# Fused causal attention and gated projection: shared output blocks, two V tiles, and new engine orders

## The chip, the cores and the metric

The kernel runs on one core of a Trainium2 chip. Its time is the device time of one execution in microseconds (us), given as the median of several runs. The engines are named as in the profile: PE does the matmuls (PEld is its weight load), DVE, ACT and POOL are the vector, scalar and GpSimd engines, and SP issues the DMAs.

## What is computed

There are 8 batches of 8 heads, 576 positions and 64 elements per head, all in float32. Attention is causal with a decay along the positions, and its result x (576 x 512 per batch) goes through a gate: a causal convolution of 5 taps per channel, a sigmoid, a product with x @ w_val, and a last projection with w_out.

```python
cum = np.cumsum(np.maximum(s, 0.0), axis=-1)
scores = q @ k.T / 8 + np.minimum(-(cum[:, None] - cum[None, :]), 0.0)   # causal
attn = exp(scores) / sum(exp(scores));  x = attn @ v                      # heads side by side
gate = sigmoid(sum(conv_w[k] * xp[k:k + S] for k in range(5)))
out = (gate * (x @ w_val)) @ w_out
```

## The kernel before

The work goes by batch b and, in a batch, by pair p of heads; n = 4b + p counts the 32 pairs. Since the decay is a difference of two terms, the part of the key is taken into V: Vp = V * w with w = exp(cum - half the total), and the part of the query falls out in the division by the sum, which is one more column of Vp.

For each batch q and k are loaded (L515; positions 512 to 575 separately as "tail", L523), cast to bf16 (L518), transposed on PE (L557, tail L546) and evacuated into QKT (L561, L549). For each pair come three score steps (L566), each with an exponential of 128x1024 on ACT (L592), and for the last 64 queries one small step per batch (exp4, L578); POOL masks the diagonal (L598, L603). Attention times Vp is L613; DVE takes the reciprocal of the sums (L618) and scales to xn (L623); PE transposes (L631) and DVE or ACT copies to xT (L635). The four older taps of the convolution, divided by the weight of the newest (the "ratios", L496 to L507), are added one by one into gp, on DVE (L647, L649) or on POOL (L644, L645). ACT takes the tanh (L653). PE does x @ w_val by halves of 288 positions and chunks of 128 channels (L660), DVE multiplies with the gate into glu (L666), PE does the last projection by blocks of positions (L672, function outp), ACT or DVE copies the block to ot (L677), and SP stores it (L680).

576 positions are four and a half blocks of 128. The kernel computes five blocks of 128 per batch, the last two overlapping (WIN, L221), and stores only the upper 64 rows of one of them: 40 blocks in all, each of four matmuls over the chunks.

V is loaded into one float32 tile, vst, in a frame whose 65th columns are 1 (L420 to L422): batch 0 by pairs of heads (L532), the others by five position blocks (L538). A load for batch b waits until the four Vp products of batch b - 1 have read the tile (L716, L717).

The order on every engine is written by a planner in the program (class Plan, L256). Each task is added with an engine, a cost in us, a key, the tasks that it needs, and the buffers that it takes and gives back. The planner runs these through a list schedule and emits the instructions in that order, so each engine's queue is fixed before the launch. Keys come from a table of offsets (DUE, L226), and for tasks that two engines can do a string of digits picks one (CHOICE, L246):

```python
t = T["xe", n] = add(("DVE", "ACT"), (0.37, 0.65), n + due("xe"), lambda e, n=n: x_evac(e, n), [t],
                     pick=("xe", n))
```

Score tasks have PE mode "R" (64 rows of the array), all others "N"; STAY (L244) is a key penalty for leaving a mode. For SP the planner lets an issue take 0.06 us and counts the transfers one after another (L352 to L355). Buffers in turn: P 3, gp 2, th 6, ot 3, qkf 3 (L389), and 8 PSUM banks.

At the end of the program a small count decides whether a general path (not taken for these inputs) is run.

Of the kernel before, what the change touches and what calls it, by code (L numbers as in the profile page):

```python
# [205 lines left out]
def pcol(kb, qb):  # L206
    if kb == qb:
        return kb * 128
    if qb == 4:
# [16 lines left out]
DUE = dict(w=-69.33, lwv=-4.26, lwo=-2.61, cwv=56.85, cwo=86.75, av=-11.07, norm=-74.98, xt=-16.64,  # L226
           xe=-86.49, tap=14.23, dtap=-1.47, tanh=-72.16, val=7.76, dval=0.88, out=11.28, dout=0.61,
           oute=87.55, qt=-4.79, qe=133.25, tt=-0.4, te=-149.08, s4=-20.03, vp=-7.1, cast=76.15, lqk=-1.56,
           mask=-123.76, lv=-49.38, av_e=7.71, av_l=6.68, cast_e=-31.51, cast_l=0.54, dout_e=-1.01,
           dout_l=-28.82, dtap_e=-7.57, dtap_l=16.17, dval_e=0.26, dval_l=0.84, lqk_e=-7.13, lqk_l=48.32,  # L230
           lv_e=98.37, lv_l=-92.01, mask_e=11.67, mask_l=11.41, norm_e=50.24, norm_l=38.99, out_e=0.39,
           out_l=42.92, oute_e=70.67, oute_l=-23.24, qe_e=-66.52, qe_l=-3.56, qt_e=4.39, qt_l=0.95,
           s4_e=8.96, s4_l=-14.16, tanh_e=58.9, tanh_l=56.45, tap_e=3.56, tap_l=-27.97, te_e=47.36,
           te_l=62.72, tt_e=19.75, tt_l=0.79, val_e=-3.44, val_l=-1.96, vp_e=-68.8, vp_l=29.32, xe_e=13.94,
           xe_l=0.22, xt_e=-5.82, xt_l=-13.61)


def due_of(b, name):
# [5 lines left out]
STAY = (0.1, 54.75)  # L244

CHOICE = dict(vp0="0100",  # L246
              cast="12200210",
              wts="00",
              te="10001100",
              qe="10100010000000001000100000100010",  # L250
              xe="00100010001000010000000000010010",
              tap="00000000100000000000001000000000000000010000100000000000000010000000000000001000001000001000100000000010000010010010001101110000",
              oute="1000001110101000010100010100011010000010")


class Plan:  # L256
# [22 lines left out]
    def run(self):  # L279
# [33 lines left out]
        while len(self.order) < len(self.tasks):  # L313
            started, later = False, []
            for e in engs:
# [36 lines left out]
                if e == "SP":  # L352
                    idle_at[e] = now + 0.06
                    dma_free = max(dma_free, now + 1.2) + us
                    t["done"] = dma_free + 0.8  # L355
                else:
                    idle_at[e] = t["done"] = now + us
# [21 lines left out]
def main_path(ctx, tc, q, k, v, s, moe_w_val, moe_conv_w, moe_w_out, out, okcnt):  # L379
# [9 lines left out]
    plan = Plan(dict(P=3, gp=2, th=6, ot=3, qkf=3))  # L389
# [30 lines left out]
    vst = one.tile([128, NKB, 8, 65], FP32, name="vst")  # L420
    nc.gpsimd.memset(vst[:, :, :, 64:65], 1.0)
    nc.gpsimd.memset(vst[0:64, 4, :, :], 0.0)  # L422
# [12 lines left out]
    glus = two("glu", [128, 4, S], BF16)  # L435
# [35 lines left out]
    t = add("DVE", 0.65, -8, relu, [t_s])  # L471
    t = add("DVE", 1.3, -8, total, [t])
    t = add("DVE", 0.75, -8, centre, [t])
# [20 lines left out]
    t = add("SP", 0.3, -8.95, lambda: nc.sync.dma_start(out=cw, in_=moe_conv_w))  # L494
    t = add("PE", 0.3, -6, conv_T, [t], take=[("bank", "cw")])
# [11 lines left out]
    t_cw = add("DVE", 1.2, -6, ratios, [t], give=[("bank", "cw")])  # L507
# [18 lines left out]
    def vprime(eng, b, p):  # L526
        h = slice(2 * p, 2 * p + 2)
        eng.tensor_tensor(Vps[b % 2][:, :, h], vst[:, :, h],  # L528
                          w[:, :, b * 8 + 2 * p:b * 8 + 2 * p + 2].unsqueeze(3).to_broadcast([128, NKB, 2, 65]),
                          ALU.mult)  # L530

    def load_v_pair(p):  # L532
        for h in (2 * p, 2 * p + 1):
            nc.sync.dma_start(out=vst[:, 0:4, h, 0:64], in_=v[0, h, 0:512, :].rearrange("(i p) d -> p i d", i=4))  # L534
        nc.sync.dma_start(out=vst[64:128, 4, HP[p], 0:64],
                          in_=v[0, HP[p], 512:576, :].rearrange("h s d -> s h d"))

    def load_v_block(b, i):  # L538
        n = kbs[i]
        nc.sync.dma_start(out=vst[128 - n:128, i, :, 0:64],  # L540
                          in_=v[b, :, kbo[i]:kbo[i] + n, :].rearrange("h s d -> s h d"))
# [127 lines left out]
    def outp(b, i):  # L669
        ps = slot["o", b, i] = bank(("o", b, i), 128, DM)  # L670
        for c in range(4):
            nc.tensor.matmul(ps, glus[b % 2][:, c, WIN[i]:WIN[i] + 128], wo[:, c, :], start=(c == 0), stop=(c == 3))  # L672

    def out_evac(e, b, i):
        r = slice(128 - kbs[i], 128)
        ot = slot["ot", b, i] = work("ot", (b, i), [128, DM], FP32)
        copy[e](ot[r, :], slot["o", b, i][r, :])  # L677

    def store(b, i):
        nc.sync.dma_start(out=out[b, kbo[i]:kbo[i] + kbs[i], :], in_=slot["ot", b, i][128 - kbs[i]:128, :])  # L680

    for b in range(B):
# [4 lines left out]
        if b == 0:  # L687
            t_tl = add("SP", 1.45, -8.4, lambda: load_tail(0))
            t_tail = T["tailc", 0] = add("DVE", 0.45, -6, lambda: nc.vector.tensor_copy(tailbs[0], tails[0]), [t_tl])
            for p in range(4):  # L690
                for wh in range(2):
                    def ld(p=p, wh=wh):
                        f = slot["f", 0, wh, p] = one.tile([128, 2, 256], FP32, name=f"first{p}{wh}")
                        dma_qk(0, wh, HP[p], f)
                    t = add("SP", 0.82, -8.5 + 0.5 * p + wh * 0.01, ld)
                    T["cast", 0, wh, p] = add(("DVE", "ACT", "POOL"), (0.32, 0.5, 0.8), p - 9, lambda e, p=p, wh=wh: cast_qk(
                        copy[e], 0, wh, HP[p], slot["f", 0, wh, p]), [t], pick=("cast", 2 * p + wh))
                t = add("SP", 1.45, -8.3 + 0.5 * p, lambda p=p: load_v_pair(p))
                T["vp", 0, p] = add(("DVE", "POOL"), (0.85, 1.25), p - 2, lambda e, p=p: vprime(
                    nc.vector if e == "DVE" else nc.gpsimd, 0, p), [t, t_w], pick=("vp0", p))  # L700
        else:
            fs = []
            for wh in range(2):
                def ld(b=b, wh=wh):
# [3 lines left out]
                c = add("POOL", 1.95, n0 + due("cast"), lambda b=b, wh=wh: cast_qk(  # L708
                    nc.gpsimd.tensor_copy, b, wh, slice(0, 8), slot["f", b, wh]),
                    [t] + [T.get(("qt", b - 2, p)) for p in range(4)], give=[("qkf", (b, wh))])  # L710
                for p in range(4):
                    T["cast", b, wh, p] = c
            t = add("SP", 1.45, n0 + due("lqk") + 0.5, lambda b=b: load_tail(b), [T.get(("tailc", b - 2))])
            t_tail = T["tailc", b] = add("POOL", 0.7, n0 + due("cast") + 0.3, lambda b=b: nc.gpsimd.tensor_copy(
                tailbs[b % 2], tails[b % 2]), [t, T.get(("tt", b - 2))])
            ts = [add("SP", 1.45, n0 + due("lv") + i * 0.01, lambda b=b, i=i: load_v_block(b, i),  # L716
                      [T["vp", b - 1, p] for p in range(4)]) for i in range(NKB)]  # L717
            for p in range(4):
                T["vp", b, p] = add("POOL", 1.25, n0 + p + due("vp"), lambda b=b, p=p: vprime(nc.gpsimd, b, p),
                                    ts + [t_w, T.get(("av", b - 2, p))])  # L720

        old_s = ([T.get(("s4", b - 2, 3))] + [T.get(("s", n0 - 8 + p, i)) for p in range(4) for i in range(3)])
        t = T["tt", b] = add("PE", 0.25, n0 + due("tt") if b else -6.5, lambda b=b: tail_T(b), [t_tail] + old_s,
                             take=[("bank", ("tt", b))])
        t_te = add(("ACT", "DVE"), (0.49, 0.6), n0 + due("te") if b else -6.3, lambda e, b=b: tail_evac(e, b), [t],
                   give=[("bank", ("tt", b))], pick=("te", b))
        for p in range(4):
            t = T["qt", b, p] = add("PE", 0.45, n0 + p + due("qt") if b else p - 6.9, lambda b=b, p=p: qk_T(b, p),
                                    [T["cast", b, 0, p], T["cast", b, 1, p]] + old_s, take=[("bank", ("qt", b, p))])
            T["qe", b, p] = add(("ACT", "DVE"), (0.9, 1.15), n0 + p + due("qe") if b else p - 6.8,  # L730
# [3 lines left out]
        for ps_ in ([[p] for p in range(4)] if b == 0 else [[0, 1, 2, 3]]):  # L734
# [7 lines left out]
            t = add("POOL", 0.15 + 0.11 * n, n0 + ps_[0] + due("mask"), lambda b=b, ps_=ps_: mask4(b, ps_), [t])  # L742
# [131 lines left out]
```

## Time and profile before

| | |
|---|---|
| median of 5 runs | 210.34 us (209.94 to 214.14) |
| the profiled execution | 209.82 us, its span 208.0 us |
| granted clock of PE, mean | 0.973 |
| PE busy | 174.1 us (84%) |
| DVE busy | 176.3 us (85%) |
| ACT busy | 163.3 us (78%) |
| POOL busy | 162.3 us (78%) |
| moved by DMA | 40.48 MB, 195 GB/s over the span |

The profile is of one execution. A row of a group gives a line of the kernel, the engine and operation, what it writes and reads with the shape of the tile, how many, and then busy us and mean ns of one. A wait is idle time of an engine ahead of an instruction, put down to what ended it. Some rows that are used later, of copies from PSUM and of the output matmuls:

| row | count | mean ns |
|---|---|---|
| L635 DVE, xT copy 128x576 | 26 | 449 |
| L635 ACT, the same | 6 | 661 |
| L561 DVE, QKT evacuation 128x1024 | 7 | 1217 |
| L561 ACT, the same | 25 | 1046 |
| L677 ACT, output copy 128x512 | 20 | 589 |
| L677 DVE, the same | 12 | 682 |
| L644 + L645 POOL, one tap | 18 | 1142 + about 1400 |
| L647 DVE, one tap | 85 | 803 |
| L672 PE, output matmul 128x512 | 141 recorded of 160 | 379 (four take 0.97 us back to back) |

### The profile page before, as it was taken

Reading aid. Unit: us, or ns where it says so; the run is one execution under the profiler, and the core shown is the slowest. Engines: PE = TensorE matmul, PEld = TensorE weight load, DVE = VectorE, ACT = ScalarE, POOL = GpSimd, SP = SyncE. Lnnn points to the kernel's source line nnn. Section 1 sums busy time; section 2 is a strip of 40 time slices with the busy share of each in tenths; the row PEclk is TensorE's granted clock in tenths of the full one; section 3 lists DMA queues with packets and bytes.
Section 4 is the critical chain, followed back from the end, with each engine's and each line's share of the span. In section 5 each row is a group of like instructions: output and inputs, shape, how many; then the busy total and the mean of one; then the engine's idle time right before and its main releaser. Section 6 shows DMA issues by size and latency. Waiting matters only on the chain.

```text
span 208.0 us, 6007 instructions
## 1 busy us (share of the span) xinstructions
PE 174.1 (84%) x2392; PEld 119.0 (57%) x2411; DVE 176.3 (85%) x311; ACT 163.3 (78%) x205; POOL 162.3 (78%) x179
## 2 busy tenths in 40 slices
PE   1598796799879997789899799989899999979950
PEld 0356584575637765467665657565576556745620
DVE  3728979999986998579999999999999998999810
ACT  2379779978997999987996997899987998553330
POOL 4276695899959987999499999958975899999300
PEclk9999969999978999999999999999999999999995
DMA  4999999999999999969997911941159120222551
GB/s 135 238 274 307 367 181 198 363 269 243 228 347 277 271 236 301 313 217 231 350 341 171 203 62 28 198 135 54 50 120 228 65 79 0 104 101 76 181 184 59
DMA packets 69230, 40.48 MB, mean 195 GB/s; under 512 B 47109, under 2 KB 63493, under 8 KB 69194
## 3 DMA queue, kind: packets, MB, share of 16 engines
q1 hardware_dynamic: 69194, 40.01, 73.0%
q8 instruction: 21, 0.34, 0.7%
q14 instruction: 15, 0.12, 0.2%
HBM read 30.57 MB, written 9.44 MB: 192 GB/s over the span
## 4 chain that ended last, share of the span: by engine, by line
DVE 29%; PE 26%; ACT 24%; issue 8%; SPq 5%; DMA 3%; POOL 2%; ACTq 0%; DVEq 0%; POOLq 0%
ACT P L592 14%; DVE gp L647 11%; PE banks L660 7%; PE banks L672 7%; PE banks L613 6%; DVE xn L623 5%; DVE gp L649 4%; DVE glu L666 4%; ACT th L653 3%; ACT QKT L561 3%; PE banks L566 2%; PE banks L631 2%; DMA first<-in_q_dram 2%; ACT ot L677 2%; SPq L534 2%
## 5 line engine op out<-in xcount | busy, mean ns | idle before, releaser
L592 ACT ACTIVATE P<-banks 128x1024 bf16<-128x1024 f32 x96 | 94.9, 1038 | 11.6 <-PE banks L566 9.7
L647 DVE SCALAR_TENSOR_TENSOR gp<-banks,ratio,gp 128x574 f32<-128x574 bf16 (+2 forms) x85 | 67.4, 803 | 2.4 <-POOL gp L645 1.7
L598 POOL TENSOR_SCALAR_AFFINE_SELECT P<-P 128x512 bf16<-128x512 bf16 x64 | 40.0, 647 | 9.6 <-ACT P L592 9.3
L566 PE MATMUL banks<-QKT 64*128 64x128 bf16 (+4 forms) x576 | 38.7, 250 | 9.0 <-ACT P L592 4.8
L660 PE MATMUL banks<-xT,wv 128*128 128x288 bf16 x256 | 41.2, 290 | 3.2 <-DVE glu L666 1.4
L672 PE MATMUL banks<-wo,glu 128*128 128x512 bf16 x141 | 38.3, 379 | 2.5 <-ACT QKT L561 0.8
L528 POOL TENSOR_TENSOR Vp<-vst,w 128x650 bf16<-128x650 f32 x29 | 37.6, 1315 | 2.0 <-DMA vst<-in_v_dram 2.0
L613 PEld LDWEIGHTS <-P 128*128 128x128 bf16 x960 | 34.6, 100 | 5.1 <-issue 2.1
L613 PE MATMUL banks<-Vp,P 128*128 128x65 bf16 x960 | 36.4, 197 | 1.3 <-ACT P L592 1.2
L566 PEld LDWEIGHTS <-QKT 64*128 64x128 bf16 x576 | 19.9, 97 | 26.7 <-issue 20.0
L660 PEld LDWEIGHTS <-wv 128*128 128x128 bf16 x256 | 22.7, 98 | 14.7 <-issue 7.3
L653 ACT ACTIVATE th<-gp,halfw 128x576 f32<-128x576 f32 x32 | 25.2, 792 | 6.3 <-POOL gp L645 3.3
L666 DVE SCALAR_TENSOR_TENSOR glu<-th,banks 128x288 bf16<-128x288 f32 x64 | 27.8, 443 | 1.5 <-PE banks L660 1.3
L561 ACT COPY QKT<-banks 128x1024 bf16<-128x1024 bf16 x25 | 25.4, 1046 | 2.4 <-PE banks L557 2.3
L623 DVE TENSOR_TENSOR xn<-banks,recs 128x640 bf16<-128x640 f32 x32 | 26.1, 817 | 0.3
L677 ACT COPY ot<-banks 128x512 f32<-128x512 f32 (+1 forms) x26 | 15.2, 587 | 11.1 <-PE banks L672 6.9
L672 PEld LDWEIGHTS <-glu 128*128 128x128 bf16 x160 | 14.6, 97 | 15.5 <-issue 2.6
L649 DVE SCALAR_TENSOR_TENSOR gp<-xT,ratio,banks 128x576 f32<-128x576 bf16 x25 | 20.1, 808 | 1.6 <-ACT xT L635 0.9
L644 POOL TENSOR_TENSOR tmp<-xT,ratio 128x576 f32<-128x576 bf16 (+3 forms) x18 | 20.6, 1142 | 0.6 <-DVE xT L635 0.2
L645 POOL TENSOR_TENSOR gp<-tmp,gp 128x573 f32<-128x573 f32 (+2 forms) x11 | 15.7, 1428 | 3.6 <-DVE gp L647 2.9
L631 PE MATMUL banks<-ident,xn 128*128 128x128 bf16 x160 | 14.1, 219 | 2.5 <-DVE glu L666 1.1
L557 PE MATMUL banks<-ident,qb 128*128 128x128 bf16 x128 | 13.5, 233 | 2.2 <-ACT qb L518 1.5
(63 smaller groups left out, 168.6 us busy)
## 6 DMA issues: line engine op xcount, KB each, us to landing
out_dram<-ot SPq DMA_DIRECT2D x32, 256.0 KB, 3.0
qkf<-in_q_dram SPq DMA_DIRECT2D x7, 1024.0 KB, 7.4
qkf<-in_k_dram SPq DMA_DIRECT2D x7, 1024.0 KB, 9.4
vst<-in_v_dram SPq DMA_DIRECT2D x28, 256.0 KB, 5.2
vst<-in_v_dram SPq DMA_DIRECT2D x15, 128.0 KB, 4.3
first<-in_q_dram SPq DMA_DIRECT2D x4, 256.0 KB, 4.0
first<-in_k_dram SPq DMA_DIRECT2D x4, 256.0 KB, 3.9
tail<-in_q_dram SPq DMA_DIRECT2D x8, 128.0 KB, 8.6
```

The source lines that it names most:

```text
L528: eng.tensor_tensor(Vps[b % 2][:, :, h], vst[:, :, h], w[:, :, b * 8 + 2 * p:b * 8 + 2 * p + 2].unsqueeze(3).to_broadcast([128, NKB, 2, 65 ...
L561: copy[e](QKTs[b % 2][:, :, p, 0:512].rearrange("d w (x j) -> d w x j", j=4), slot["qt", b, p].rearrange("d w (j x) -> d w x j", j=4))
L566: nc.tensor.matmul(ps[:, hh, c0:c0 + nq], QKTs[b % 2][r, 1, p, k0:k0 + 128], QKTs[b % 2][r, 0, p, q0:q0 + nq], **kw)
L592: nc.scalar.activation(out=slot["Pt", n][:, :, step * 512:(step + 1) * 512], in_=slot["s", n, step], func=AF.Exp, scale=0.125)
L598: nc.gpsimd.affine_select(out=d, in_=d, pattern=[[0, 4], [1, 128]], compare_op=ALU.is_ge, fill=0.0, base=0, channel_multiplier=-1)
L613: nc.tensor.matmul(ps[:, hh, qb * 65:qb * 65 + 65], lhsT, Vps[b % 2][:, kb, 2 * p + hh, :], start=(kb == 0), stop=(kb == qb))
L623: nc.vector.tensor_tensor(xns[b % 2][:, :, p * 128:(p + 1) * 128].rearrange("t g (h d) -> t h g d", h=2), pv[:, :, :, 0:64], recs[:, n].un ...
L647: nc.vector.scalar_tensor_tensor(gp[:, o:S], slot["x", n][:, 0:S - o], r, gp[:, o:S], ALU.mult, ALU.add)
L653: nc.scalar.activation(out=th, in_=slot["g", n], func=AF.Tanh, scale=halfw[:, n % 4, :])
L660: nc.tensor.matmul(ps, wv[:, dc, c * 128:(c + 1) * 128], xTs[b % 2][:, dc, 2 + o:290 + o], start=(dc == 0), stop=(dc == 3))
L666: nc.vector.scalar_tensor_tensor(glus[b % 2][:, c, o], slot["t", n][:, o], 1.0, slot["v", n, hf], ALU.add, ALU.mult)
L672: nc.tensor.matmul(ps, glus[b % 2][:, c, WIN[i]:WIN[i] + 128], wo[:, c, :], start=(c == 0), stop=(c == 3))
```

## The change

- **Nine output blocks per two batches.** The gate products of an even and the next odd batch lie in one tile of 1152 positions, and the projection takes nine full blocks of it; the block in the middle has 64 positions of each batch and belongs to the odd one. So there are 36 blocks in place of 40, and each is stored whole.
- **The last projection by chunks.** In the last batch each block's four matmuls are four tasks, one per chunk of channels, so that a chunk can be done when its gate product is there.
- **Two V staging tiles.** Batches alternate between them; a load waits for the products of two batches back. Batch 1 is loaded by pairs of heads. The second tile first serves as landing place for five of the eight first q and k loads, and gets its frame (two memsets on POOL) after their casts.
- **Ratios later.** The transposition of the conv weights waits for a cast of the third pair, and the ratios follow it.
- **Five ot buffers** in place of three.
- **Planner.** SP's issue is held back once more than BEHIND us of transfers are queued; costs of some POOL tasks are changed (Vp 1.25 to 1.33, mask 0.6 to 0.635, a tap 2.25 to 2.5); the keys of the start become entries of DUE; some more tasks can choose their engine; DUE, STAY and CHOICE have new values. With them DVE does 17 xT copies (26 before), 5 QKT evacuations (7), 13 output copies (14), and 110 taps as before.

```diff
+BEHIND = 11.28
-                    idle_at[e] = now + 0.06
                     dma_free = max(dma_free, now + 1.2) + us
+                    idle_at[e] = max(now + 0.06, dma_free - BEHIND)
...
-    plan = Plan(dict(P=3, gp=2, th=6, ot=3, qkf=3))
+    plan = Plan(dict(P=3, gp=2, th=6, ot=5, qkf=3))
...
+    vraw = [one.tile([128, NKB * 8 * 65], FP32, name=f"vst{j}") for j in range(2)]
+    vsts = [a.rearrange("p (i h d) -> p i h d", i=NKB, h=8) for a in vraw]
+    def v_frame(j):
+        nc.gpsimd.memset(vsts[j][:, :, :, 64:65], 1.0)
+        nc.gpsimd.memset(vsts[j][0:64, 4, :, :], 0.0)
+    v_frame(0)
...
-    glus = two("glu", [128, 4, S], BF16)
+    glu2 = one.tile([128, 4, 2 * S], BF16, name="glu")
+    glus = [glu2[:, :, 0:S], glu2[:, :, S:]]
...
-    def outp(b, i):
-        ps = slot["o", b, i] = bank(("o", b, i), 128, DM)
-        for c in range(4):
-            nc.tensor.matmul(ps, glus[b % 2][:, c, WIN[i]:WIN[i] + 128], wo[:, c, :], start=(c == 0), stop=(c == 3))
+    def outp(b, i, cs):
+        if cs[0] == 0:
+            slot["o", b, i] = bank(("o", b, i), 128, DM)
+        o = (4 * (b % 2) + i) * 128
+        for c in cs:
+            nc.tensor.matmul(slot["o", b, i], glu2[:, c, o:o + 128], wo[:, c, :], start=(c == 0), stop=(c == 3))
...
-        nc.sync.dma_start(out=out[b, kbo[i]:kbo[i] + kbs[i], :], in_=slot["ot", b, i][128 - kbs[i]:128, :])
+        r = b // 2 * 2 * S + (4 * (b % 2) + i) * 128
+        nc.sync.dma_start(out=outf[r:r + 128, :], in_=slot["ot", b, i])
...
+            if b == 1:
+                t = add("POOL", 0.7, DUE["vf"], lambda: v_frame(1), [T["cast", 0, i % 2, i // 2] for i in range(5)])
+                ts = [[add("SP", 1.45, DUE["lv1"] + DUE["lv1d"] * p, lambda p=p: load_v_pair(1, p), [t])] for p in range(4)]
+            else:
+                ts = [[add("SP", 1.45, n0 + due("lv") + i * 0.01, lambda b=b, i=i: load_v_block(b, i),
+                           [T["vp", b - 2, p] for p in range(4)]) for i in range(NKB)]] * 4
...
+            t = add("PE", 0.3, DUE["cvt"], conv_T, [t_lcw, T["cast", 0, 1, 2]], take=[("bank", "cw")])
+            t_cw = add("DVE", 1.2, DUE["rat"], ratios, [t], give=[("bank", "cw")])
...
-        for i in range(NKB):
+        for i in range(4 + b % 2):
+            own = [(0,), (0,), (0, 1), (1,), (1,)][i]
+            need = lambda c: [T["glu", n0 + c, hf] for hf in own] + ([T["glu", n0 - 4 + c, 1]] if b % 2 and i == 0 else [])
+            if b == B - 1:
+                t = None
+                for c in range(4):
+                    t = add("PE", 0.22, n0 + DUE["ol"] + DUE["old"] * i + DUE["doc"] * c, lambda b=b, i=i, c=c: outp(b, i, (c,)),
+                            need(c) + [t_wo, t or T["xt", n0 + 3], T["val", n0 + 2, 1]], take=[] if c else [("bank", ("o", b, i))])
+                T["out", b, i] = t
```

The new strings of engines, where they differ most (a digit 1 is ACT for xe, DVE for qe and oute, POOL for tap):

```diff
-              qe="10100010000000001000100000100010",
-              xe="00100010001000010000000000010010",
+              qe="00000000000100010100010000000001",
+              xe="00111001110111000001000001101011",
...
-              oute="1000001110101000010100010100011010000010")
+              oute="0011101000001000101010100111100000001000")
```

## Prediction, made before the run

> **What bounds the kernel now.** I began with the stretches of the span, because shares over the whole span mix a start, a middle and an end. The columns are busy us (and instructions) of each engine, the granted clock, and the busy share of the DMA engines.
>
> ```profile
> 0.00:20.80 20.80, 12.80 (x139) 8.95 (x140) 11.34 (x23) 12.17 (x17) 11.44 (x28) 1.00 0.88 238
> 20.80:93.60 72.80, 61.84 (x938) 43.98 (x941) 63.67 (x107) 65.46 (x81) 62.65 (x63) 0.95 1.06 272
> 93.60:178.80 85.20, 78.91 (x1176) 54.10 (x1187) 82.96 (x150) 76.20 (x94) 73.36 (x79) 1.00 0.56 142
> 178.80:187.20 8.40, 7.25 (x77) 4.73 (x75) 8.33 (x15) 3.81 (x6) 7.93 (x7) 1.00 0.32 122
> 187.20:208.00 20.80, 13.27 (x77) 7.22 (x78) 10.05 (x20) 5.64 (x9) 6.94 (x6) 0.90 0.37 125
> ```
>
> The order is PE, PEld, DVE, ACT, POOL. In the third row, the second half of the attention work, DVE is busy 82.96 of 85.20 us (97%), PE 93%, ACT 89%, POOL 86%: DVE bounds it, with little room behind it. In the second row nobody is above 90% (ACT): four engines wait for each other in turn. The chain that ended last says the same, with no engine holding a third:
>
> ```profile
> DVE 29%; PE 26%; ACT 24%; issue 8%; SPq 5%; DMA 3%; POOL 2%; ACTq 0%; DVEq 0%; POOLq 0%
> ```
>
> Next the waits (total us, times, longest), cut to those that the change touches:
>
> ```profile
> PEld L566 <- issue: 20.0, 53, 0.9
> ACT P L592 <- PE banks L566: 9.7, 16, 1.1
> ...
> ACT ot L677 <- DMA out_dram<-ot: 2.7, 2, 1.5
> ...
> POOL Vp L528 <- DMA vst<-in_v_dram: 2.0, 3, 1.0
> ```
>
> The first is the weight load of a score matmul standing 0.38 us each time that PE comes to scores from other work. The third is the last batch's evacuations waiting until one of three ot buffers has been stored. The fourth says that V arrives in time nearly always: a second V tile has at most 2.0 us to give, on an engine that is not the bound. Last, the end of the timeline (start, duration):
>
> ```profile
> 175.93 2.83 ACT L592 ACTIVATE P<-banks 128x1024 bf16<-128x1024 f32 x3
> ...
> 181.65 0.82 DVE L623 TENSOR_TENSOR xn<-banks,recs 128x640 bf16<-128x640 f32 x1
> ...
> 194.94 1.81 DVE L666 SCALAR_TENSOR_TENSOR glu<-th,banks 128x288 bf16<-128x288 f32 x4
> ...
> 196.09 4.48 PE L672 MATMUL banks<-wo,glu 128*128 128x512 bf16 x19
> ...
> 201.90 0.59 ACT L677 COPY ot<-banks 128x512 f32<-128x512 f32 x1 [1.45 <-DMA out_dram<-ot]
> ```
>
> The last exponential ends at 178.76 and the span at 208.0: 29.2 us of tail, in four pieces: to the last norm's end at 182.47 (3.7), DVE from there to the last gate product at 196.75 (14.3), to the last evacuation's end at 202.49 (5.7), the last store (5.5).
>
> **What moves, engine by engine.** I counted each engine's tasks in both orders and priced them by the rows of before.
> - DVE: 9 xT copies fewer (26 to 17) x 0.449 = -4.0; 2 QKT evacuations x 1.217 = -2.4; 2 first casts x 0.42 = -0.8; one Vp product -0.8; one output evacuation -0.7; one tail evacuation +0.4. Sum -8.4 us, 176.3 to 167.9.
> - ACT takes most of it: +9 x 0.661 = +5.9; 2 QKT x 1.046 = +2.1; one cast +0.6; 3 output evacuations x 0.587 = -1.8; one tail evacuation -0.6. Sum +6.3, 163.3 to 169.6.
> - POOL: one Vp product +1.3, one cast +0.6, the second V tile's frame +0.7 (its two memset rows, 0.16 and 0.52). Sum +2.6, 162.3 to 164.9. The 18 taps on POOL and 110 on DVE stay as many; only 4 instead of 6 of POOL's stand after the last mask, 5 us moved ahead of it.
> - PE: 40 output blocks become 36, 4 x 4 matmuls x 0.24 (four take 0.97 back to back) = -3.9. And PE goes over to the scores 51 times instead of 63. The row prices an entry at 0.38: 12 x 0.38 = -4.6. The Trainium skill, "TensorEngine Tiling (Array Packing)", section "Key Properties", says that changing the tiling mode drains the engine; the scores use 64 rows, all else 128, so I take the wait as that drain. If it were only the weights' own lateness, hidden under running matmuls, the 4.6 would be nothing: the bounds are 0 and 4.6, and PE counts for little in what follows.
>
> The copies are where a rule and a row differ. "VectorE: DVE Perf Modes", section "Specifications", puts ScalarE closer to PSUM and VectorE closer to SBUF, and its cycle table (section "The TRN2 errata — SBUF-src ops pay a fixed extra latency per instruction") gives, without a perf mode, (120+576)/0.96 = 725 ns for this PSUM copy on DVE and (172+576)/1.2 = 623 on ACT, which are estimates from that page. By it nine moved copies would save 0.9 us of engine time in all. The rows are 449 on DVE (bf16 in and out) and 661 on ACT: the move costs 1.9 us and pays only if DVE is the scarcer. I go by the rows.
>
> **Start.** SP now issues the conv weights, two tail loads, then q and k of the first pair; before, s, the weights, then q and k. Two tail issues took 0.69 + 0.63, and s 0.60 falls behind: the first q is issued about 0.8 later (2.01 to 2.8). The first exponential, at 9.37 before, comes at about 10.3. But then three follow at once, since the tail part is already there, where before ACT stood idle between them; s comes 3 us later, its scan (1.35) and centring (0.83) are on DVE before the first Vp product is wanted. From there ACT's queue up to the twelfth exponential holds 12 x 0.98, three QKT evacuations, three casts, w and three small ones, 18.7 us, so it ends at 29.0 instead of 27.4, but with one cast and two QKT evacuations more and one tanh less done (1.9 us). The ratios (seven ops, 1.07 us from 5.21 to 6.28, in a gap of DVE) now stand between the first xT copy and the first tap; behind them on DVE are the taps, and for these ACT's tanh. DVE has 12% to spare in that stretch. The transposition ahead of them on PE waits for a cast that is done by then, with the first x transposition behind it. Start: 0, bounds -1 and +1.5.
>
> **Middle.** Two readings. By total work: -8.4 +6.3 +2.6 -8.5 = -8.0 us over four engines, -2.0 each, which at the mean busy share of before (676.0 of 832, 81%) is -2.5 in the whole span; the tail below holds most of that, so the middle gets -0.3. By the busiest engine up to the last exponential and norm: DVE had 161.4 of its work there, ACT 153.7; now DVE 153.4 and ACT 159.9, the greater falls by 1.5. I take -1.0. Cover that may go: in the third stretch, cut in both orders behind pair 14's exponentials, ACT gets 4 QKT and 4 xT copies more, 2 output copies fewer (+5.6 on 76.2: 96% of 85.2), so each late xT copy now holds exponentials behind it, and POOL 1.9 more. Bounds -5 and +7 (the rivals).
>
> V: the same bytes, but batch 1's by twelve DMAs instead of five behind one block of batch 2's (about 0.9 us at 272 GB/s); nothing waits on SP that is due before. The frame waits for five casts. Hidden by that 2.0 us row: 0, bounds -1 and +1.
>
> **Tail.** Last exponential to last norm: 3.7, as before. DVE from there: an output copy 0.7, the check 2.84, 5 + 8 products x 0.44, 6 taps x 0.81 = 14.2; the same sum for before is 15.2 where the trace took 14.3, so 13.8 here, between. POOL's four taps end about 10.2 after the mask at 178.2, in time for the tap that follows. Then: the order has 3 of the last batch's 20 output matmuls ahead of the third chunk's product, so 17 x 0.224 (4.48 for 20) = 3.8 are left, from 0.44 before the last product; with an evacuation 0.6 and the handover this is 4.05 instead of 5.7. With five ot buffers the waits of 1.26 and 1.45 are gone; what is late next is PE itself. Tail 27.0, -2.2; bounds -3 and -1.
>
> **The sum.** 208.0 + 0 - 1.0 - 2.2 = 204.8 of span. The profiled execution took 209.82, so 1.8 lies outside the span, and the median 210.34 is 0.5 above it: 204.8 + 2.34 = 207.1.
>
> **Rivals.**
> 1. The order packs well (0.20). If ACT reaches the 97% that DVE shows in the third row, its 157.3 us from the first to the last exponential (159.9 less the table load, the first QKT and a small exponential) take 162.2: 10.3 + 162.2 + 27.0 = 199.5, time 201.8. For it: DVE had it, and its relief removes ACT's 9.7 us of waiting for scores if PE is freer. Against: no engine got there while a second stood at 96%.
> 2. ACT becomes the bound and keeps its waits: slower (0.22). Before, ACT had 151.4 us of work between the first exponential (9.37) and the last (178.76) and was idle 18 there. If the copies that it takes over, each waiting for PE and for a norm on DVE, keep 18: 10.3 + 157.3 + 18 + 27.0 = 212.6, time 214.9. It decides from an idle time of 13.4 us on, where the span is 208.0 again.
> 3. Nothing but the tail, and the middle gives it back (0.16): more work on ACT and POOL (+5.6 and +1.9 in the third stretch) against less on DVE before it; 207 to 209, time about 210.
>
> The likeliest, 0.42, has its own range of 205.0 to 209.2. With the part of 1 that lies above 202, 3, and 2 up to 213, the range is 202.0 to 213.0. Half a per cent is about what a measurement of this kernel tells from no change (209.3 to 211.4): faster 0.62, within 0.16, slower 0.22.
>
> **What would show it.** First exponential at about 10.3; DVE busy near 168 and ACT near 170; scores' weight loads waiting 15 to 16 us in place of 20.0; no ACT wait for a store in the tail; last exponential at about 177.8 and 27 us after it. I am wrong if ACT waits for xT or QKT inputs longer than the 2.3 us of before, or if the last exponential is later than 181.

## The result, and the profile after

The changed kernel took 213.37 us (median of 26 runs) where the kernel before took 210.34 (47 runs beside it). Its time is 1.0069 times that of before, 95% interval 1.0041 to 1.0097: slower by 0.7%, where 207.1 us was forecast. Medians here are over all runs; the ratios leave out runs more than 1.5% above the fastest of their kernel (half of the changed kernel's), so 1.0069 is less than the two medians make. The profiled execution took 212.50 us, its span 210.7, at a granted clock of 0.948.

The five stretches of the span again, the same borders except the last end (columns: PE, PEld, DVE, ACT, POOL busy us and instructions, granted clock, DMA share, GB/s):

```profile
0.00:20.80 20.80, 10.42 (x135) 7.58 (x136) 6.85 (x13) 11.23 (x15) 12.83 (x29) 1.00 0.87 216
20.80:93.60 72.80, 56.89 (x814) 39.10 (x816) 59.96 (x101) 62.29 (x79) 60.89 (x64) 0.90 1.00 265
93.60:178.80 85.20, 79.30 (x1229) 57.25 (x1239) 80.61 (x144) 79.79 (x101) 77.02 (x80) 0.98 0.57 151
178.80:187.20 8.40, 8.27 (x110) 5.22 (x111) 8.36 (x16) 5.50 (x7) 7.44 (x7) 1.00 0.17 64
187.20:210.70 23.50, 15.44 (x97) 9.16 (x97) 13.49 (x26) 8.83 (x14) 6.43 (x5) 0.90 0.38 138
```

The loss is in the second row. It is as long as before, but every engine got less done in it: PE 56.9 us instead of 61.8, DVE 60.0 instead of 63.7, ACT 62.3 instead of 65.5, and the clock there fell from 0.95 to 0.90. Nobody is the bound in it, everybody waits more. The chain names a load that it did not name before (by engine):

```profile
PE 26%; DVE 23%; ACT 17%; POOL 8%; DMA 8%; issue 8%; SPq 6%; DVEq 0%; ACTq 0%; POOLq 0%
```

DMA went from 3 to 8%, half of it (4% of the span) the load of q. The waits:

```profile
PEld L581 <- issue: 24.2, 55, 1.3
ACT QKT L576 <- PE banks L572: 11.0, 4, 7.0
...
PE banks L581 <- ACT P L607: 8.6, 18, 1.1
POOL qb L532 <- DMA qkf<-in_q_dram: 8.1, 2, 5.1
```

The first was to fall to 15 or 16 us and rose from 20.0 to 24.2; what it is made of is told further down. The last is two q casts, one of which stood 5.1 us for its load. And the tail:

```profile
197.15 2.99 DVE L681 SCALAR_TENSOR_TENSOR glu<-th,banks 128x288 bf16<-128x288 f32 x8
...
199.36 4.48 PE L690 MATMUL banks<-wo,glu 128*128 128x512 bf16 x19
...
203.92 0.59 ACT L694 COPY ot<-banks 128x512 f32<-128x512 f32 x1 [0.28 <-PE banks L690]
```

The last evacuation waits 0.28 us for PE and no longer 1.45 for a store. Set against each other by the ends of the exponentials:

| us | before | forecast | after |
|---|---|---|---|
| first exponential | 9.37 | 10.3 | 10.86 |
| those of pair 3 end | 27.3 | 29.0 | 29.4 |
| those of pair 8 end | 61.3 | | 64.1 |
| those of pair 14 end | 92.4 | | 96.4 |
| last one ends | 178.8 | 177.8 | 184.5 |
| from there to the end | 29.2 | 27.0 | 26.2 |

The forecast span was 204.8 and the measured one 210.7. Of the 5.9 between, 0.4 were there by pair 3, 6.3 came between pair 3 and the last exponential, and the tail gave 0.8 back. Up to pair 14 the delay is 4 us; from pair 15 (104.1 us against 98.2) to the last one it stays at some 5.8. So the late half of the kernel, which the forecast looked at most, is not where it was lost.

### The profile page after: what moved, and what is told of

It is laid out like the page before. It is cut to its first block, busy times and chain, and to the rows that moved or that the text cites. A ratio compares the mean times of both kernels' runs of the same rounds, so it can differ in the third digit from the quotient of the medians.

```text
span 210.7 us, 5956 instructions
## 1 busy us (share of the span) xinstructions
PE 170.3 (81%) x2376; PEld 118.3 (56%) x2395; DVE 169.3 (80%) x297; ACT 167.6 (80%) x213; POOL 164.6 (78%) x183
## 4 chain that ended last, share of the span: by engine, by line
PE 26%; DVE 23%; ACT 17%; POOL 8%; DMA 8%; issue 8%; SPq 6%; DVEq 0%; ACTq 0%; POOLq 0%
ACT P L607 10%; PE banks L690 8%; PE banks L675 6%; DVE gp L662 5%; PE banks L628 5%; DMA qkf<-in_q_dram 4%; DVE xn L638 4%; ACT QKT L576 4%; POOL Vp L542 4%; DVE gp L664 3%; PE banks L581 3%; DVE glu L681 3%; PE banks L572 2%; POOL P L613 2%; DMA tail<-in_k_dram 2%
## 5 line engine op out<-in xcount | busy, mean ns | idle before, releaser
L662 DVE SCALAR_TENSOR_TENSOR gp<-banks,ratio,gp 128x573 f32<-128x573 bf16 (+2 forms) x81 | 64.0, 805 | 0.8
L675 PE MATMUL banks<-xT,wv 128*128 128x288 bf16 x256 | 38.7, 287 | 1.5 <-DVE gp L662 0.5
L576 ACT COPY QKT<-banks 128x1024 bf16<-128x1024 bf16 x27 | 27.2, 1035 | 12.7 <-PE banks L572 11.0
L581 PEld LDWEIGHTS <-QKT 64*128 64x128 bf16 x576 | 19.4, 98 | 31.8 <-issue 24.2
L690 PE MATMUL banks<-wo,glu 128*128 128x512 bf16 x125 | 35.0, 388 | 1.8 <-DVE glu L681 0.4
L675 PEld LDWEIGHTS <-wv 128*128 128x128 bf16 x256 | 23.1, 97 | 11.3 <-issue 4.5
L638 DVE TENSOR_TENSOR xn<-banks,recs 128x640 bf16<-128x640 f32 x32 | 26.2, 820 | 0.6
L664 DVE SCALAR_TENSOR_TENSOR gp<-xT,ratio,banks 128x576 f32<-128x576 bf16 x29 | 23.1, 800 | 0.5
L660 POOL TENSOR_TENSOR gp<-tmp,gp 128x574 f32<-128x574 f32 (+2 forms) x15 | 21.1, 1403 | 1.3 <-DVE gp L664 0.2
L694 ACT COPY ot<-banks 128x512 f32<-128x512 f32 x23 | 13.7, 596 | 9.3 <-PE banks L690 9.2
L659 POOL TENSOR_TENSOR tmp<-xT,ratio 128x574 f32<-128x574 bf16 (+3 forms) x18 | 20.6, 1145 | 0.4
L532 POOL CAST qb<-qkf 128x2048 bf16<-128x2048 f32 x7 | 13.3, 1893 | 8.1 <-DMA qkf<-in_q_dram 8.1
L572 PE MATMUL banks<-ident,kb 128*128 128x128 bf16 x128 | 14.1, 240 | 3.4 <-POOL kb L532 3.3
```

The costliest lines, as they stand in the source:

```text
L576: copy[e](QKTs[b % 2][:, :, p, 0:512].rearrange("d w (x j) -> d w x j", j=4), slot["qt", b, p].rearrange("d w (j x) -> d w x j", j=4))
L581: nc.tensor.matmul(ps[:, hh, c0:c0 + nq], QKTs[b % 2][r, 1, p, k0:k0 + 128], QKTs[b % 2][r, 0, p, q0:q0 + nq], **kw)
L638: nc.vector.tensor_tensor(xns[b % 2][:, :, p * 128:(p + 1) * 128].rearrange("t g (h d) -> t h g d", h=2), pv[:, :, :, 0:64], recs[:, n].un ...
L662: nc.vector.scalar_tensor_tensor(gp[:, o:S], slot["x", n][:, 0:S - o], r, gp[:, o:S], ALU.mult, ALU.add)
L664: nc.vector.scalar_tensor_tensor(gp, xs[:, 1:1 + S], r, slot["x", n], ALU.mult, ALU.add)
L675: nc.tensor.matmul(ps, wv[:, dc, c * 128:(c + 1) * 128], xTs[b % 2][:, dc, 2 + o:290 + o], start=(dc == 0), stop=(dc == 3))
```

## What could have done it

Reading the two traces gives three theories.

**A, late loads.** SyncE issues batch 2's q after batch 1's V. In the trace of before, then of after (start, duration of SP's issues):

```profile
25.97 7.18 SPq L540 DMA_DIRECT2D vst<-in_v_dram  x5
33.25 0.57 SPq L483 DMA_DIRECT2D qkf<-in_moe_w_out_dram  x1
33.92 0.45 SPq L515 DMA_DIRECT2D qkf<-in_q_dram  x1
```

```profile
27.06 2.35 SPq L555 DMA_DIRECT2D vst<-in_v_dram  x1
29.46 2.00 SPq L549 DMA_DIRECT2D vst<-in_v_dram  x2
...
38.03 0.60 SPq L550 DMA_DIRECT2D vst<-in_v_dram  x1
38.73 0.54 SPq L499 DMA_DIRECT2D qkf<-in_moe_w_out_dram  x1
39.37 0.45 SPq L529 DMA_DIRECT2D qkf<-in_q_dram  x1
```

Five V transfers took SP 7.2 us; the early block of batch 2 and twelve transfers by pairs take 11.6, and q is issued 5.45 us later. On POOL the cast then waits:

```profile
48.69 1.89 POOL L532 CAST qb<-qkf 128x2048 bf16<-128x2048 f32 x1 [5.11 <-DMA qkf<-in_q_dram]
```

The same cast began at 46.06 before, with no wait.

**B, the moved copies.** ACT took over nine xT copies, each behind a norm and a transposition, and holds exponentials behind them (my second rival).

**C, the clock.** PE's granted clock is half in three stretches of the work of after (at 25.1, 55.9 and 90.0 us, 17.1 us in all) and in two of before (26.2 and 60.3 us, 6.8). Cut at their borders, after:

```profile
21.70:25.10 3.40, 1.59 (x24) 0.80 (x22) 3.30 (x10) 3.19 (x6) 2.00 (x2) 1.00 1.07 355
25.10:31.90 6.80, 5.67 (x63) 4.43 (x60) 4.84 (x5) 6.80 (x9) 6.72 (x8) 0.50 1.17 237
52.50:55.90 3.40, 1.38 (x25) 1.39 (x26) 0.65 (x1) 0.95 (x2) 3.33 (x4) 1.00 1.01 182
55.90:59.30 3.40, 3.07 (x20) 1.55 (x19) 2.70 (x4) 2.91 (x4) 3.32 (x5) 0.50 1.06 185
86.60:90.00 3.40, 1.40 (x20) 0.71 (x18) 3.29 (x5) 3.40 (x6) 3.25 (x4) 1.00 1.09 354
90.00:96.80 6.80, 5.68 (x63) 4.27 (x63) 4.66 (x8) 6.59 (x9) 6.27 (x7) 0.50 1.05 311
```

Each half-clock stretch follows 3.4 us in which PE (first column) was busy 1.4 to 1.6 us, that is 41 to 47%; ACT beside it was busy nearly throughout in the first and third. There the new order gives PE a long run of score steps, and each step waits for a bank that ACT frees once per exponential:

```profile
87.22 0.40 PE L581 MATMUL banks<-QKT 64*128 64x128 bf16 x8 [0.41 <-ACT P L593]
88.14 0.39 PE L581 MATMUL banks<-QKT 64*128 64x64 bf16 x4 [0.52 <-ACT P L607]
89.59 0.39 PE L581 MATMUL banks<-QKT 64*128 64x320 bf16 x4 [1.06 <-ACT P L607]
```

A step is 0.4 us of work in some 0.95. The tasks that were held back meanwhile come in a bunch, and meet the half clock: 30 attention matmuls took 1.86 us at 93.81 and 1.07 at 97.01. Counted by weight loads in the traces, the longest runs of score matmuls of after are 36 (from 22.3 us) and 32 (from 86.7), and of other matmuls (the end left out) 136 (from 92.9) and 134; before has 28 (from 11.4) and then 18, and 90. The thin window at 52.5 has another reason: there PE waits for the late q and k, so A feeds C.

## The experiments

The kernels ran in three groups, each with its own runs of the kernel before: the first four (median of before 210.12), the next four (211.01), the last four (210.08). Ratios from different groups are compared with up to 0.8% of doubt: kernels 10, 11 and 12 of the last group are 1, 7 and 5 with little changed, and their ratios are 0.7 to 0.8% higher. The last column is the median of the granted clock over the runs.

| kernel | median us (runs) | to before, 95% | clock |
|---|---|---|---|
| before | 210.34 (47) | 1 | 0.973 |
| changed | 213.37 (26) | 1.0069 (1.0041 to 1.0097) | 0.956 |
| 1 V by blocks | 211.43 (14) | 0.9988 (0.9947 to 1.0030) | 0.949 |
| 2 xT copies as before | 216.46 (6) | 1.0284 (1.0220 to 1.0347) | 0.942 |
| 3 orders as before | 236.27 (6) | 1.1193 (1.1131 to 1.1255) | 0.930 |
| 4 = 1 and 2 | 214.29 (6) | 1.0175 (1.0112 to 1.0239) | 0.938 |
| 5 = 1, scores twice | 208.55 (6) | 0.9863 (0.9821 to 0.9906) | 0.986 |
| 6 changed, scores twice | 211.17 (22) | 1.0002 (0.9972 to 1.0032) | 0.976 |
| 7 before, five ot | 209.22 (6) | 0.9853 (0.9797 to 0.9909) | 0.978 |
| 8 changed, three ot | 226.30 (4) | 1.0728 (1.0674 to 1.0782) | 0.925 |
| 9 V by blocks, one in front | 211.50 (22) | 1.0044 (1.0018 to 1.0070) | 0.948 |
| 10 = 1, scores twice elsewhere | 211.89 (22) | 1.0060 (1.0029 to 1.0091) | 0.947 |
| 11 = 7, scores twice | 208.82 (10) | 0.9935 (0.9895 to 0.9975) | 0.984 |
| 12 = 5, a wait filled | 208.88 (22) | 0.9944 (0.9919 to 0.9970) | 0.982 |

### 1 and 9: batch 1's V by blocks

```diff
-    lambda p=p: load_v_pair(1, p)
+    lambda p=p: load_v_one(p)      # at p == 3: load_v_block(1, i) for the five i
-    lambda b=b, i=i: load_v_block(b, i)
+    lambda b=b, i=i: load_v_later(b, i)   # (2, 0) is issued ahead of (2, 1); not in 9
```

The places in the order are otherwise kept.

> The changed kernel with its planned order kept, but batch 1's V loaded by five block transfers in place of twelve pair transfers, and batch 2's first V block moved behind batch 2's q and k. Theory A (late loads: q and k of batch 2 were issued at 39.4 us instead of 33.9, and four engines waited for them): they are issued near 34 us again, POOL's cast no longer waits 5.1 us, the ninth pair's exponentials end about 2.5 us sooner, the whole is 2 to 4 us faster than the changed kernel (ratio to the kernel before near 0.99). Theory B (ACT is the bound, with the copies it took over holding its exponentials): the wait goes but is made up by ACT, less than 1 us.

> The changed kernel with only batch 1's V changed back to five block transfers; batch 2's first V block stays in front of them (the version with both moved took 211.43). The q of batch 2 was issued at 39.37 us in the changed kernel and at 36.50 with both moved. If the number of transfers is what delays it, five blocks of some 1.4 us in place of twelve transfers give q at about 37.2 and most of the gain: 211.7 to 212.2. If the one block in front (2.35 us of SyncE) is what delays it: q at 38.5 or later and about 213.

```profile
29.01 6.72 SPq L555 DMA_DIRECT2D vst<-in_v_dram  x5
35.83 0.58 SPq L499 DMA_DIRECT2D qkf<-in_moe_w_out_dram  x1
36.50 0.46 SPq L529 DMA_DIRECT2D qkf<-in_q_dram  x1
```

That is SP in kernel 1: q goes out 2.9 us earlier than in the changed kernel (not at 34 us, as expected), and its cast begins at 47.53 instead of 48.69, with no wait for q. Against that stands a new wait, of 3.1 us, of a product of V for batch 1's V. The ratio falls from 1.0069 to 0.9988, 0.8% or 1.7 us where 2 to 4 were expected. The two intervals are apart, but the groups differ. Inside one group the same edit is what divides kernels 6 and 5 (below): 1.0002 and 0.9863, 1.4% or 2.9 us, with the intervals well apart. So A holds, for some 1.7 to 2.9 us.

In kernel 9 q is issued at 37.74: of the 2.9 us, 1.6 come from the twelve transfers and 1.2 from the early block. But there the early block stands in front of batch 1's V, and V is what POOL now waits for:

```profile
41.03 5.00 POOL L542 TENSOR_TENSOR Vp<-vst,w 128x650 bf16<-128x650 f32 x4 [5.11 <-DMA vst<-in_v_dram]
```

In the traces the exponentials of pairs 4 to 8 take 34.7 us in the changed kernel and in kernel 9, and 32.6 in kernel 1. So the twelve transfers alone are not the fault, the early block has its part. By the times this is not settled: kernel 9's ratio lies between the two others and its median beside that of kernel 1.

### 2 and 4: the copies back on their engines

```diff
     plan.total = plan.run()
+    # every xT copy is emitted on the engine that CHOICE "xe" of before gives it, at its place in the order
```

> The changed kernel with its planned order kept, but each xT copy done by the engine that did it before (6 on ACT and 26 on DVE in place of 15 and 17). Theory B (ACT bounds it): ACT has 6 us less to do, DVE 4 us more; the last exponential comes 2 to 4 us sooner. Theory A (late loads): the wait for q and k is untouched, within 1 us of the changed kernel; or slower by 1 to 3 us, since DVE is at 97% in the second half and the copies now stand in its queue.

> Both edits of the first two at once. If they act on different waits, their gains add; by theory A alone it is as the first, by theory B alone as the second.

Both are slower, by 2.1% without the blocks and 1.9% with them. DVE, which has nine copies more, is no busier for it per us (171.9 of 214.4, 80%), and other waits grow, the first two in kernel 2:

```profile
PEld L581 <- issue: 25.9, 60, 1.5
ACT QKT L576 <- PE banks L572: 16.3, 5, 6.6
```

Theory B falls: in this order the copies belong on ACT, and putting them back costs about 2%. What a plan made anew with the copies on DVE would take isn't told, since both kernels keep the places that were planned for ACT. Kernel 4 against 2 (same group) points to A once more, 1.1% this time, though their intervals overlap.

### 3: the structure with the orders of before

```diff
-DUE, CHOICE, STAY, BEHIND   # values of after
+DUE, CHOICE, STAY           # of before, with keys for the new tasks of the start; BEHIND off
```

> The changed kernel's structure (nine blocks per two batches, chunked last projection, two V tiles, five ot buffers, later ratios) with the keys, engine choices and mode penalties of before, planned with these. If the new orders are what costs: 2 to 4 us faster than the kernel before, by the tail (2.2) and four blocks fewer. If the structure itself costs (two V tiles and their loads): no faster than before.

12% slower than the kernel before. Keys found for one set of tasks and buffers did not carry over to another here, and what the structure alone is worth isn't told by this run.

### 5, 6 and 10: score matmuls issued twice

To test C without moving anything I gave PE needless work in its thin windows: the matmuls of 19 score steps are issued twice, the second time with the same result into the same bank.

```diff
-        for m, (kb, q0, nq, c0) in enumerate(STEPS[step]):
+        for _ in range(2 if (n, step) in TWICE else 1):
+            for m, (kb, q0, nq, c0) in enumerate(STEPS[step]):
```

In 5 and 6 TWICE holds pairs 2, 3, 10, 13 and 14, and steps 11/0, 11/1, 12/1, 12/2; in 10, the control, pairs 20 to 25 and 26/0.

> The first experiment (batch 1's V by blocks) and, in three stretches where PE does nothing but scores at ACT's pace (pairs 2 and 3, 10 and 11, 12 to 14: 19 score steps), every score matmul done twice with the same result, which adds about 0.4 us of PE work per step beside an idle PE. Theory C (PE's clock is halved after a stretch in which it is busy half the time or less, and the bunch of projections behind it then runs at half speed): the half-clock stretches near 25, 69 and 90 us go, the granted clock rises from 0.95 to 0.97 or more, and the time falls 1 to 2 us below the first experiment (ratio about 0.99) although PE does more. Rival (the clock costs nothing, other engines bound): no gain, or up to 1 us slower by the added work.

> The changed kernel with only the doubled score matmuls in the 19 steps. Theory C: 1 to 2 us faster than the changed kernel; the wait for q and k of batch 2 and the half clock behind it (near 56 us) stay. Rival: as the changed kernel or slower.

> A control for the doubled scores: batch 1's V by blocks as in the version of 211.43, and again 19 score steps with their matmuls issued twice, but at pairs 20 to 25 and the first step of 26, where no window was at half clock and TensorE was 74 to 98% busy. If the doubled matmuls helped at pairs 2, 3 and 10 to 14 (208.55) because they keep the clock up, they can help nothing here and cost up to 19 times 0.39 = 7.4 us where TensorE sets the pace, nothing where ScalarE does: 211.5 to 216. If doubling helps for some other reason, such as denser entries into score matmuls, it helps here too: about 209.

Kernel 5 does more work than kernel 1 and takes 1.25% less time, about 2.6 us (across two groups). The windows ahead of and in what was the third stretch, in kernel 5:

```profile
85.60:89.00 3.40, 2.27 (x44) 1.47 (x39) 2.60 (x4) 3.40 (x6) 3.40 (x5) 1.00 1.06 356
89.00:92.40 3.40, 2.51 (x43) 1.53 (x40) 3.36 (x6) 3.40 (x5) 3.13 (x4) 1.00 1.09 350
```

PE is busy 67 and 74%, and the clock stays at 1.00. Kernel 10 has as many doubled steps where the clock was full anyway, keeps the thin windows, and takes 211.89 us at a clock of 0.947, as kernel 1 does. So it is the place of the work, not the doubling as such, that helps: theory C. Kernel 6 does the same to the changed kernel without the blocks: the ratio falls by 0.67% or 1.4 us, its interval just apart from that of the changed kernel, but inside the doubt between groups. Kernels 12 and 10 are of one group: 0.9944 and 1.0060, 1.2% or 2.4 us. Some 0.9 us of that is what the control's doubled steps cost it: in the traces the exponentials of pairs 20 to 26 take 36.6 us in kernel 10 and 35.7 in 1 and 12. So C is worth 1.4 to 2.6 us.

What one stretch costs can be read in the traces. Here are ACT's last exponential of pair 14 and the three of pair 15 in the changed kernel, then in kernel 5:

```profile
95.23 1.12 ACT L607 ACTIVATE P<-banks 128x1024 bf16<-128x1024 f32 x1
...
101.19 2.88 ACT L607 ACTIVATE P<-banks 128x1024 bf16<-128x1024 f32 x3
```

```profile
94.49 1.11 ACT L620 ACTIVATE P<-banks 128x1024 bf16<-128x1024 f32 x1
...
98.64 2.88 ACT L620 ACTIVATE P<-banks 128x1024 bf16<-128x1024 f32 x3
```

From end to end that is 7.7 and 5.9 us, with the same four copies of ACT between. The same for before and for the kernels of the new order that keep these copies (us between the ends of the exponentials, one execution each; kernels 3 and 8, slow for reasons of their own, are left out):

| | before | changed | 1 | 9 | 10 | 5 | 6 | 12 |
|---|---|---|---|---|---|---|---|---|
| pair 3 to pair 8 | 33.9 | 34.7 | 32.6 | 34.7 | 31.4 | 33.0 | 35.7 | 32.0 |
| pair 14 to pair 15 | 5.8 | 7.7 | 7.8 | 7.0 | 7.2 | 5.9 | 5.9 | 5.9 |
| half clock near 90 us | 0 | 6.8 | 6.8 | 3.4 | 3.4 | 0 | 0 | 0 |

The second row goes with the third: 1.1 to 1.3 us for 3.4 us at half clock, 1.8 to 1.9 for 6.8. This third stretch is most of what C is worth; of the stretches near 25 and 56 us no such price can be read. The first row goes with the V loads: 34.7 us and more where the early block was left in front (changed, 9, 6), 33.0 and less in the others of the new order. Kernel 1 loses most of its gain there again in pairs 9 to 11, which take 19.0 us in place of 17.2: its profile has a half-clock stretch at 69.0 us that the changed kernel's has not.

### 12: one more thin window

Kernel 5 still has a half-clock stretch at 54.8 us, behind PE's 2.1 us of waiting for the cast of k.

```diff
-        for which in range(2):
+        for which in ([0] * 5 + [1] if (b, p) == (2, 0) else [0, 1]):
```

> The version of 208.55 (batch 1's V by blocks, 19 score steps issued twice), and the four transposes of batch 2's first q pair issued five times in place of once, which puts about 1.5 us of matmul into the 2.1 us in which TensorE waits for the k cast at 51.7 to 53.8. If the half clock that follows at 54.8 us (3.4 us) is caused by the thin window and costs time, it goes, and the time falls to 207.3 to 208.0. If it is hidden behind the late k, the time stays at 208.3 to 208.9.

The stretch at 54.8 is gone from the profile, but one of 6.8 us came at 36.2, behind a window that was 46% busy; on kernel 5's grid the windows at that place were 59 to 68% busy. The median is 208.88 against 208.55, in different groups: no gain to be seen, and whether a removed stretch there is worth anything stays open.

### 7 and 8: the number of ot buffers

```diff
-        ot = slot["ot", b, i] = work("ot", (b, i), [128, DM], FP32)
+        ot = slot["ot", b, i] = one.tile([128, DM], FP32, name=f"ot{turn[0] % K}")   # K = 5 (7), 3 (8)
+        turn[0] += 1
```

> The kernel before with five ot buffers in turn in place of three, its order kept. By the prediction's tail, the waits of 1.26 and 1.45 us for stores go and the end comes 1.3 us sooner (ratio 0.994). If the last stores bound the end anyway (the transfers just queue later), no gain.

> The changed kernel with three ot buffers in turn in place of five, its order kept. If the buffers carry part of the tail's gain: 1 to 2 us slower than the changed kernel, with evacuations waiting for stores at the end. If not: the same.

In the kernel before, five buffers alone take the waits for stores away (tail 28.2 instead of 29.2 us) and give 209.22 us, a ratio of 0.9853 where 0.994 was expected. The tail accounts for 1.0 us of it; the rest isn't explained, rests on six runs, and kernel 11, with the same buffers in another group, has 0.9935. In the changed kernel three buffers cost 6.5%:

```profile
DVE ot L697 <- DMA out_dram<-ot: 11.1, 1, 11.1
PE banks L628 <- DVE ot L697: 9.5, 1, 9.5
```

One copy on DVE stands 11 us for a store, and PE and all behind them with it. The order was planned with five buffers, so "three" is no fair measure of what they bring in it; kernel 7 is.

### 11: the same cure for the kernel before

> The kernel before with five output buffers in turn (209.22), and the score matmuls of nine steps issued twice: 2/2, 3/0 to 3/2, 4/0, 7/2 and 8/0 to 8/2, which lie in its two windows of 52 and 62% busy, each followed by 3.4 us at half clock (27.2 and 61.4 us). If the half clock costs time in the order of before as well, both stretches go, and with them up to half of 3.4 us each, part of it under other waits: 207.2 to 208.5. If these stretches lie in slack (its exponentials at pair 3 were not late), no gain: 209 to 210.

The edit is that of 7 with nine doubled steps. Both stretches are gone from the profile (another, of 3.4 us, came at 32.8). The median is 208.82 against 209.22, at the border of the two expectations, but the ratio 0.9935 against 0.9853, in different groups: nothing that the runs can tell from no change. So this kernel does not show that the half clock costs anything in the order of before.

## Why the prediction was wrong

The step that failed is the middle, from pair 3's exponentials to the last one: 148.8 us by the forecast, 155.1 measured. It had V's loads at 0 and PE's clock not at all, and looked for the cost of the new order on ACT and POOL. What the runs showed is q and k of batch 2 late behind V's transfers (1.7 to 2.9 us) and PE at half clock behind runs of scores (1.4 to 2.6 us). Both of the prediction's own signs of being wrong came: ACT's QKT copies waited 11.0 us for PE, and the last exponential ended at 184.5, later than 181.

**Tail: right.** Forecast 29.2 to 27.0, measured 26.2, at the edge of its bounds. The pieces: to the last norm 3.0 (3.7 forecast), DVE from there to the last gate product 12.6 (13.8), to the last evacuation's end 4.4 (4.05), the store 6.2 (5.5). No wait for a store is left, and PE is what is late next, as forecast. By kernel 7 the buffers make 1.0 of the 3.0 us; how much is the chunks' and how much the missing blocks' was not tested.

**Work of the engines: right.** DVE 169.3 us (forecast 167.9), ACT 167.6 (169.6), POOL 164.6 (164.9). PE fell by 3.8 to 170.3 (3.9 from the blocks alone). The estimate from the cycle table would have made the copies' move a gain of engine time; the rows gave a loss of 1.9 us, and kernel 2 bears out that the copies are better on ACT in this order all the same. The prediction took that table without a perf mode. With a multiplier of 2, the same table of the Trainium skill ("VectorE: DVE Perf Modes", section "The TRN2 errata — SBUF-src ops pay a fixed extra latency per instruction") gives (120 + 288)/0.96 = 425 ns for the copy on DVE, an estimate close to the 449 of the row.

**V: wrong.** "The same bytes [...] nothing waits on SP that is due before [...] Hidden by that 2.0 us row: 0." The 2.0 us row tells only what waits for V. Behind the V transfers in SP's queue stood the q and k of batch 2, and the wait came out on them: 5.1 us of POOL, and 1.7 to 2.9 us of the time. The bound of +1 was too narrow too.

**PE: wrong, in the sign of what matters.** "The row prices an entry at 0.38: 12 x 0.38 = -4.6 [...] and PE counts for little in what follows." The entries did fall from 63 to 51, but the row was misread. Of its 53 waits before, 30 (10.0 us) stand where PE comes to the scores, and 23 (10.0 us) inside a run of scores. In the trace of after, one of each kind, with the row of PE beside the second:

```profile
85.41 0.45 PEld L581 LDWEIGHTS <-QKT 64*128 64x128 bf16 x16 [0.42 <-issue]
...
89.59 0.23 PEld L581 LDWEIGHTS <-QKT 64*128 64x128 bf16 x4 [1.33 <-issue]
89.59 0.39 PE L581 MATMUL banks<-QKT 64*128 64x320 bf16 x4 [1.06 <-ACT P L607]
```

At the entries the profile, which models the ends of matmuls, has PE's matmuls under way through all but 0.1 us of the waits in both traces, so they cost PE next to nothing: the prediction's own lower bound, 0, was the right one. The second is the scores' waiting for a bank. After, the entries' waits are 27 (8.4 us) and those inside 28 (15.8 us): the rise of the row is the gathered scores standing for ACT. By the trace they made two of the three thin windows. The forecast left the clock out and took over the 0.973 of before; measured, it is 0.956 over the runs. I had the half-clock stretches of before in the profile's clock row, and did not ask what set them.

**Start: off.** It was to be 0 net, with bounds -1 and +1.5. The exponentials of pair 3 end 2.1 us later than before, near the 29.0 forecast, but the work that was to be ahead in exchange is not: in the first 20.8 us ACT did 11.2 us of work instead of 12.2, and DVE 6.9 instead of 11.3.

**Middle: wrong.** -1.0 forecast, and between pair 3 and the last exponential 155.1 us against 151.5 before. With A and C taken away (kernels 5 and 12) the traces have 151.6 and 151.0 there: 3.5 to 4.1 of the 6.3 that it is over the forecast. By the ratios the two kernels are 2.6 to 4.3 us faster than the changed one, and 0.4 to 2.1 above the forecast. What that rest is wasn't tested. Against before, two places stand out in their traces: the start, and pairs 9 to 14, which take 32.3 to 32.7 us against 31.2.

**The rivals.** The second, "ACT becomes the bound and keeps its waits", has the idle time nearly to the tenth: ACT has 155.4 us of work between first and last exponential (157.3 forecast for it) and is idle 18.25 (18), and the span is 210.7 (212.6). But its reason, the copies that ACT takes over, is not borne out by kernel 2, so the close number is luck. By A and C, ACT keeps its idle time because PE, late with q and then running at half clock, keeps it waiting. An idle time that stays the same while its causes change is no evidence for a cause.

## What to carry to other kernels

When a transfer is cut into more pieces or moved forward, list what stands behind it in that queue and when it is due; the waits for the moved data itself do not tell it. When an order gathers the short, paced work of PE into runs, look at PE's busy share in windows of 3.4 us: here each one that left it more than half idle was followed by half clock, and one such stretch slowed the dense work behind it by 1.1 to 1.9 us. And keep in mind that planned keys can belong to the buffers and tasks that they were planned with: kernels 3 and 8 are 11 and 6.5% slower than the changed kernel by mixing. Last, a row of waits adds up waits of different kinds: before pricing one, look at single instructions of it.

## What the chip showed that was not expected

**Half clock without an idle window.** In all 14 profiles here the granted clock changes at borders of a grid of 3.413 us, and the records begin 16 to 24 us into the span. I cut the time from there to 200 us into those windows and took the share in which PE had a matmul or a weight load under way. Of 678 windows at full clock, those under 50% busy (27, of which two, in kernel 8, were nearly idle) were all followed by a window at half clock, those from 50 to 65% (42) in 9 cases, those above 65% (609) never. It came out of half clock where a window was at least 81% busy, and stayed in it up to 78%. The Trainium skill, "TensorE: Matmul & The Clock Gate", section "A second HAM failure mode: psum-queue depth-cycling", says that short idle gaps of PE between groups of matmuls can be enough to make the clock go up and down; the runs agree, and add the share at which it happens here.

**The grid moves from run to run.** The stretches of one and the same order lie elsewhere in each profile (kernels 5 and 12 above), since the windows do not start with the kernel. In the kernel before, of the 109 runs in the three groups, 24 at a granted clock of 0.98 or more have a median of 208.96 us, 65 at 0.97 to 0.98 210.41, 15 at 0.96 to 0.97 211.02, and 5 below that 213.25 (correlation -0.69). In the changed kernel's own 28 runs the relation is weak (-0.32), so its times spread for other causes too.

**More matmuls, less time.** Kernel 5, with its doubled score steps, is the changed kernel's best form. With 0.9863 (0.9821 to 0.9906), and in kernel 12 0.9944 (0.9919 to 0.9970), it is faster than both kernels; so is the kernel before with five output buffers.
